# Storing the last pair of token blocks by column halves on three queues, with its last quarter scaled on VectorE

## The chip, the cores and the metric

The kernel runs on one core of a Trainium2 chip. The metric is device time in microseconds (us). It exceeds the span of the profile, which runs from the first to the last instruction, by about 1.7 us. Runs spread over about half a microsecond.

In the traces TensorE is PE and runs the matmuls; VectorE is DVE and ScalarE is ACT, which do the arithmetic on their results; GpSimd is POOL and SyncE is SP. A store is a DMA, a copy to memory. SyncE, ScalarE and GpSimd each start DMAs from a queue of their own. An *issue* is the time for which starting one holds that engine; a store *lands* when its data has arrived; its *flight* here counts from the start of the issue to the landing. "+0.42" is 0.42 us after the end of the last matmul.

## The reference

```python
def _attn_ref(q, k, v, phi):          # batch 8, heads 8, seq 576, head_dim 64, 32 memory slots
    ...                               # softmax of phi makes k_m and v_m; softmax of q k_m^T; times v_m
def _moe_ref(x, w_a, w_b, w_out):     # x: 4608 tokens x 512
    a = x @ w_a
    b = x @ w_b
    return (a * b @ w_out).astype(np.float32)   # 4608 x 512 f32
```

Only the end matters here: the product with `w_out`, its scaling, and the stores of the result.

## The kernel before

Two blocks of 128 tokens are multiplied with `w_out` together, in seven products of half size. They leave four quarters of 128 x 256: left and right columns of block one (`o1`) and of block two (`o2`). `store` sends a block as two halves of 64 rows, each a DMA of its own. For the last pair (`ends`) block two already goes by column halves.

```python
def store(o_sb, cidx, cs=slice(0, d_model), engines=(nc.sync, nc.sync)):
    pair, c = divmod(cidx, NI)
    for z in range(2):
        slot = 2 * c + z
        engines[z].dma_start(out=out_rows[2 * pair + slot // NI, slot % NI, :, cs], in_=o_sb[64 * z:64 * z + 64, cs])
...
        plus(o1[:, NH:], v, u2)                     # quarter 1: block one, right (VectorE)
...
        plus(o2[:, NH:], y, u5)                     # quarter 2: block two, right
        if ends:
            store(o2, cidx + 1, slice(NH, d_model))
...
        plus(o1[:, :NH], x, u1)                     # quarter 3: block one, left
        store(o1, cidx)
...
        nc.scalar.mul(out=o2[:, :NH], in_=y, mul=scale)   # quarter 4: block two, left
        if ends:
            store(o2, cidx + 1, slice(0, NH), (nc.sync, nc.scalar))
```

The softmax here doesn't subtract the row's maximum and nothing guards it: scores larger than these inputs give would overflow.

## Time and profile before

| | before |
|---|---|
| time, median | 247.86 us (247.41 to 247.93) |
| span of the profile | 246.2 us |
| TensorE busy | 95% of the span |
| last matmul ends | 241.4 us |
| last quarter ready | 241.85 us |
| SyncE's last store issued | 243.08 us |

The rows to compare are the last two: a store waits 1.23 us for its turn on a queue while its data lies ready. The prediction shows the lines. The chain of waits on the page does not show this, because it ends at the last compute instruction.

### The profile page before, as it was taken

The numbers are of one execution on the slowest core, as the hardware profiler recorded it, in microseconds if no ns is written. First come the engines' busy times: TensorE is split into PE (matmuls) and PEld (weight loads), VectorE is DVE, ScalarE is ACT, GpSimd is POOL, SyncE is SP. The second block draws the span as 40 slices with busy tenths as digits, with TensorE's granted clock in tenths as the row PEclk, the third lists the DMA queues.
The fourth block names the chain that finished last, engine by engine and source line by source line (L and its number), as shares of the span: only waits on it lengthen the run. The fifth ranks groups of instructions, "written<-read, shape, count | busy, mean of one in ns | idle before, by whom it ended". The sixth has DMA issues, their size and how long they took to land.

```text
span 246.2 us, 7624 instructions
## 1 busy us (share of the span) xinstructions
PE 233.1 (95%) x3016; PEld 165.7 (67%) x3016; DVE 168.6 (68%) x405; ACT 158.6 (64%) x410; POOL 152.8 (62%) x124
## 2 busy tenths in 40 slices
PE   7589999999998999999999999999999999999992
PEld 2334574456665857777787777877787878888881
DVE  3454784468959968876994559865996586756651
ACT  2364772678697489578856768587856867465430
POOL 8734263499799028892899759892849087946000
PEclk9855999999999999999999999999999999999999
DMA  6999999999969804973159832696120303033253
GB/s 202 209 197 207 209 254 206 256 217 284 225 174 209 165 3 105 235 134 88 27 137 216 184 85 44 160 201 160 35 53 3 85 12 77 19 72 75 45 129 95
DMA packets 26035, 33.81 MB, mean 137 GB/s; under 512 B 1936, under 2 KB 20368, under 8 KB 26000
## 3 DMA queue, kind: packets, MB, share of 16 engines
q0 software_dynamic: 19280, 22.71, 50.5%
q1 hardware_dynamic: 6368, 9.97, 16.3%
q10 hardware_dynamic: 352, 0.66, 0.7%
q8 instruction: 23, 0.38, 0.6%
q14 instruction: 12, 0.10, 0.1%
HBM read 42.47 MB, written 9.44 MB: 211 GB/s over the span
## 4 chain that ended last, share of the span: by engine, by line
PE 89%; DVE 3%; DMA 3%; ACT 2%; issue 1%; DVEq 0%
PE pa L584 21%; PE pb L594 19%; PE py L462 16%; PE pv L462 8%; PE pva L337 6%; PE po L389 5%; PE px L462 4%; DMA phi_sb<-in_phi_dram 3%; PE pkv L213 2%; PE pD L314 2%; PE pscore L292 2%; PE pk L256 2%; PE pT L274 1%; PE pT L242 1%; ACT a_sb L587 1%
## 5 line engine op out<-in xcount | busy, mean ns | idle before, releaser
L597 DVE TENSOR_TENSOR ht<-a_sb,pb 128x288 f16<-128x288 f16 x192 | 83.0, 449 | 41.9 <-ACT a_sb L587 28.7
L587 ACT CAST a_sb<-pa 128x288 f16<-128x288 f32 x192 | 75.0, 406 | 31.6 <-PE pa L584 29.3
L584 PE MATMUL pa<-A,vab 128*128 128x288 f16 x384 | 77.4, 291 | 1.6 <-DVE A L325 1.1
L594 PE MATMUL pb<-A,vab 128*128 128x288 f16 x384 | 77.2, 289 | 0.7 <-ACT vab L349 0.5
L444 POOL TENSOR_TENSOR h_sums<-ht 128x768 f16<-128x768 f16 x28 | 45.8, 1639 | 38.8 <-DVE ht L597 37.3
L594 PEld LDWEIGHTS <-vab 128*128 128x128 f16 x384 | 37.5, 99 | 13.4 <-issue 1.7
L584 PEld LDWEIGHTS <-vab 128*128 128x128 f16 x384 | 34.9, 99 | 16.1 <-issue 8.7
L462 PEld LDWEIGHTS <-h_sums 128*128 128x128 f16 x384 | 37.4, 98 | 6.9 <-issue 0.4
L349 ACT CAST vab<-pva 128x512 f16<-128x512 f32 (+1 forms) x52 | 28.0, 559 | 12.0 <-PE pva L337 12.0
L349 DVE CAST vab<-pva 128x512 f16<-128x512 f32 (+1 forms) x52 | 32.6, 643 | 2.9 <-PE pva L337 2.2
L462 PEld LDWEIGHTS <-ht 128*128 128x128 f16 x288 | 28.1, 98 | 5.6 <-issue 0.4
L462 PE MATMUL py<-w_sums,h_sums 128*128 128x256 f16 x192 | 30.3, 272 | 0.0
L444 POOL TENSOR_TENSOR h_sums<-h_sums,ht 128x768 f16<-128x768 f16 x14 | 23.1, 1647 | 1.0
L444 POOL TENSOR_TENSOR h_sums<-ht,h_sums 128x768 f16<-128x768 f16 x14 | 23.0, 1640 | 1.0
L305 ACT ACTIVATE E<-pscore 128x288 f16<-128x288 f32 x32 | 11.4, 417 | 11.3 <-PE pscore L292 11.2
L325 POOL TENSOR_TENSOR A<-E,R 128x576 f16<-128x576 f16 x10 | 12.8, 1275 | 7.1 <-ACT R L323 6.8
L462 PE MATMUL py<-wo_sb,ht 128*128 128x256 f16 x96 | 16.0, 273 | 0.0
L462 PE MATMUL pv<-w_sums,h_sums 128*128 128x256 f16 x96 | 16.0, 272 | 0.0
L469 ACT ACTIVATE u<-py 128x256 f32<-128x256 f32 x32 | 12.4, 387 | 5.2 <-PE py L462 5.0
L462 PE MATMUL py<-w_sums,ht 128*128 128x256 f16 x96 | 15.5, 272 | 0.1
L462 PE MATMUL px<-wo_sb,ht 128*128 128x256 f16 x96 | 15.4, 273 | 0.0
L204 DVE STREAM_TRANSPOSE qT<-q_sb 128x288 f32<-128x288 f32 x32 | 14.3, 462 | 0.6 <-DMA q_sb<-in_q_dram 0.6
(62 smaller groups left out, 262.7 us busy)
## 6 DMA issues: line engine op xcount, KB each, us to landing
out_dram<-o_sb SPq DMA_DIRECT2D x70, 128.0 KB, 2.6
kv_sb<-in_v_dram POOLq DMA_DIRECT2D x7, 576.0 KB, 10.4
phi_sb<-in_phi_dram POOLq DMA_DIRECT2D x7, 576.0 KB, 4.7
kv_sb<-in_k_dram POOLq DMA_DIRECT2D x7, 576.0 KB, 8.2
q_sb<-in_q_dram POOLq DMA_DIRECT2D x6, 576.0 KB, 13.4
wo_sb<-in_moe_w_out_dram POOLq DMA_DIRECT2D x3, 512.0 KB, 16.3
q_sb<-in_q_dram POOLq DMA_DIRECT2D x4, 288.0 KB, 12.6
wa_sb<-in_moe_w_a_dram POOLq DMA_DIRECT2D x2, 512.0 KB, 14.9
```

The source lines that it names most:

```text
L204: nc.vector.transpose(out=t["qT"][:, hp, :].bitcast(F32), in_=qs[b][:, hp, :].bitcast(F32))
L325: engine.tensor_tensor(out=attn[b][:, g, sl], in0=t["E"][:, g, sl], in1=t["R", g][:, sl], op=ALU.mult)
L337: nc.tensor.matmul(t["pva", lo, z][g][0][32 * j:32 * j + 32, 0:hi - lo], t["kvT"][64 * r:64 * r + 64, 4 + g, M * j:M * j + M], w_sbs[z][64 ...
L349: engine_copy(out=vabs[b][z][:, g, lo:hi], in_=pva[:, 0:hi - lo])
L389: nc.tensor.matmul(po, ht[:, i, P * c:P * (c + 1)], wo_sb[:, i, :], start=(i == 0), stop=(i == NFF - 1))
L444: engine.tensor_tensor(out=out, in0=in0, in1=in1, op=op)
L462: nc.tensor.matmul(po, lhs[:, i], rhs[:, i], start=first and i == 0, stop=i == KH - 1, skip_group_check=not first)
L469: nc.scalar.mul(out=x, in_=po, mul=scale)
L584: nc.tensor.matmul(pa, vab[0][:, g, fs], A[:, g, HALF * hf:HALF * (hf + 1)], start=(g == 0), stop=(g == 1))
L587: nc.scalar.copy(out=a_sb, in_=pa)
L594: nc.tensor.matmul(pb, vab[1][:, g, fs], A[:, g, HALF * hf:HALF * (hf + 1)], start=(g == 0), stop=(g == 1))
L597: nc.vector.tensor_tensor(out=ht[:, i, t0:t0 + HALF], in0=a_sbs[hf - hfs[0]], in1=pb, op=ALU.mult)
```

## The change

Its intent is to shorten the tail after the last matmul. Each quarter leaves as soon as it is ready, no queue has a backlog when the last quarter comes, and ScalarE, which now issues stores, doesn't scale the last quarter. This is the whole diff, with unchanged lines left out at `...`.

```diff
         plus(o1[:, NH:], v, u2)
+        if ends:
+            store(o1, cidx, slice(NH, d_model), (nc.gpsimd, nc.gpsimd))
         ...
         plus(o2[:, NH:], y, u5)
         if ends:
-            store(o2, cidx + 1, slice(NH, d_model))
+            store(o2, cidx + 1, slice(NH, d_model), (nc.sync, nc.scalar))
         ...
         plus(o1[:, :NH], x, u1)
-        store(o1, cidx)
+        if ends:
+            store(o1, cidx, slice(0, NH), (nc.sync, nc.scalar))
+        else:
+            store(o1, cidx)
         ...
-        nc.scalar.mul(out=o2[:, :NH], in_=y, mul=scale)
+        if ends:
+            nc.vector.tensor_scalar(out=o2[:, :NH], in0=y, scalar1=scale, scalar2=None, op0=ALU.mult)
+        else:
+            nc.scalar.mul(out=o2[:, :NH], in_=y, mul=scale)
```

## The prediction

> **What bounds the kernel now.** I read the page first, then the timeline of the last ten microseconds, then the DMA issues one at a time, and last the stretches after the final matmul.
>
> The page's share of busy time and its chain say that TensorE sets the pace through the body.
>
> ```profile
> PE 233.1 (95%) x3016; PEld 165.7 (67%) x3016; DVE 168.6 (68%) x405; ACT 158.6 (64%) x410; POOL 152.8 (62%) x124
> ...
> ## 4 chain that ended last, share of the span: by engine, by line
> PE 89%; DVE 3%; DMA 3%; ACT 2%; issue 1%; DVEq 0%
> ```
>
> The change touches neither a matmul nor anything ahead of the last pair of token blocks. I compared the two programs' instruction order engine by engine: TensorE has the same rows in the same order, and the differences on the others are in the last few instructions. So 240 of the 246.2 us should not move. The page's chain also stops too early for this question: it ends at the last compute instruction (ScalarE's L508), and the stores that follow it are not in it. The timeline has them (columns: start us, length us, engine, line, operation, tiles, count; idle time and its releaser in brackets).
>
> ```profile
> 239.51 0.42 DVE L473 SCALAR_TENSOR_TENSOR o_sb<-pv,u 128x256 f32<-128x256 f32 x1 [1.89 <-ACT u L469]
> ...
> 240.14 0.42 DVE L473 SCALAR_TENSOR_TENSOR o_sb<-py,u 128x256 f32<-128x256 f32 x1 [0.20 <-PE py L462]
> 240.62 0.81 PE L462 MATMUL py<-w_sums,ht 128*128 128x256 f16 x6
> 240.79 0.42 DVE L473 SCALAR_TENSOR_TENSOR o_sb<-px,u 128x256 f32<-128x256 f32 x1 [0.23 <-PE px L462]
> 241.47 0.38 ACT L508 ACTIVATE o_sb<-py 128x256 f32<-128x256 f32 x1 [2.23 <-PE py L462]
> 241.88 0.55 ACTq L451 DMA_DIRECT2D out_dram<-o_sb  x1
> ```
>
> The four quarters of the last pair are ready at 239.93, 240.56, 241.21 and 241.85 us. The span is 246.2, so 4.4 us pass after the last quarter is ready. SyncE's issues, read one by one, say what fills them:
>
> ```profile
> 240.59 0.47 SPq L451 DMA_DIRECT2D out_dram<-o_sb  x1
> 241.10 0.60 SPq L451 DMA_DIRECT2D out_dram<-o_sb  x1
> 241.80 0.54 SPq L451 DMA_DIRECT2D out_dram<-o_sb  x1
> 242.38 0.60 SPq L451 DMA_DIRECT2D out_dram<-o_sb  x1
> 243.08 0.54 SPq L451 DMA_DIRECT2D out_dram<-o_sb  x1
> ```
>
> In order these are the two halves of the right quarter of block two, the two full-width halves of block one, and the first half of the left quarter of block two. Each takes 0.58 to 0.70 us of the sequencer with its gap, except the first at 0.51. Block one was ready at 241.21 but is issued at 241.80 and 242.38. The last quarter was ready at 241.85, but its SyncE half is issued at 243.08, 1.23 us late. Only its ScalarE half went out at once (241.88).
>
> The DMA issues in the last 5.7 us give the time from issue to landing, and the waits of SyncE over the same end say that it is these landings that close the program:
>
> ```profile
> out_dram<-o_sb SPq DMA_DIRECT2D x2, 128.0 KB, 2.4
> out_dram<-o_sb SPq DMA_DIRECT2D x3, 64.0 KB, 2.0
> out_dram<-o_sb ACTq DMA_DIRECT2D x1, 64.0 KB, 2.5
> ...
> SPq L710 <- DMA out_dram<-o_sb: 1.1, 3, 0.5
> ```
>
> So the last one lands at 243.08 + 2.0 = 245.1. The other 246.2 - 245.1 = 1.1 us are SyncE stepping through the remaining completion semaphores and the closing barrier. The end is therefore 241.85 (data ready) + 1.23 (queue of SyncE) + 2.0 (flight) + 1.1 (close). The change can only take from the second term and disturb the third.
>
> **What the Trainium skill says.** "DMA: Bandwidth & Descriptors", section "Issuing engines are not separate DMA queues", says that DMAs from all engines share the same 16 DMA engines and that issuing from several saves the sequencer's time alone. That is just the term in question here, and the trace agrees that it is not small at this place: 1.23 us of 4.4. The same page's "Anatomy of one DMA" gives about 2.0 us of fixed cost; the 64 KB stores of the trace show 2.0 us in all, and 2.5 for the one from ScalarE. "VectorE: DVE Perf Modes", section "Why PSUM operands drop a tier", says an fp32 operand from PSUM runs at 1x. The trace agrees: VectorE's 128x512 and 128x256 PSUM casts take 684 and 421 ns, a slope of 263/256 = 1.03 ns per column. "SBUF — State Buffer", section "SBUF: two separate sides", warns that a two-port VectorE operation starves descriptor writing on GpSimd. VectorE's operations at 239.5 to 241.9 have an operand in PSUM, so I expect none; no trace shows it yet.
>
> **The change part by part.**
>
> 1. *Block one, right quarter, to GpSimd.* Ready at 239.93, two issues from 239.96. GpSimd's issues in this trace take about 0.75 us each, so they are done near 241.5. For the load of phi issued at 155.70, the packet records show the first data 1.55 us after the issue's start. So data at about 241.5 and 242.3. For a SyncE store of 64 KB the packets take 0.45 us and the semaphore 0.35 more, so my estimate is a landing by 243.1: not last. GpSimd is otherwise idle there.
>
> 2. *Block two, right quarter, over SyncE and ScalarE.* Both issue at 240.59. SyncE is free at 241.06 in place of 241.70.
>
> 3. *Block one, left quarter, over both.* Ready at 241.21, issued at about 241.24 on both and done at 241.8. The wait of 0.59 us goes, and a full-width 2 x 128 KB becomes 2 x 64 KB here.
>
> 4. *The last quarter scaled on VectorE.* ScalarE took 0.38 us. VectorE should take 0.42: that is what the 128x256 f32 combination and the 128x256 cast from PSUM both take. It costs 0.04 us, and the data is ready at 241.89. What it avoids is ScalarE standing in its own way: its issue of part 3 holds its sequencer until 241.8, and the scaling could not start at 241.47.
>
> 5. *The last two issues.* Both at about 241.92, in place of 243.08 on SyncE. The issue is 1.16 us earlier.
>
> If flight and close stayed at 2.0 and 1.1, the span would fall by 1.16 us. But flight will not be 2.0 for both halves. The bytes are the same 512 KB in less time, and two 64 KB pieces arrive at once: by the packet records one 1 KB packet takes some 0.07 us, so 64 packets on 16 engines are 0.28 us, and two pieces side by side add about 0.2 to the later. And ScalarE's store landed 2.5 us after issue, not 2.0; its first packet came 1.7 us after the issue against SyncE's 1.1. At the start of the kernel the same pair of queues, both issued at 0.81 us, had first packets at 1.93 and 2.72, so ScalarE is again the later by 0.8. With 2.5 for its half the last landing is 241.92 + 2.5 = 244.4 and the gain 245.1 - 244.4 = 0.7 us. I take 0.7 as the middle: 247.86 - 0.7 = 247.1 us after rounding down.
>
> **Rivals.**
>
> *Free queues.* ScalarE's 2.5 was only contention with block one's 2 KB packets: the stretch 243.5 to 244.1 shows the DMA full.
>
> ```profile
> 243.50:244.10 0.60, 0.00 (x0) 0.00 (x0) 0.00 (x0) 0.00 (x0) 0.00 (x0) 1.00 1.05 321
> ```
>
> (The last two columns are the DMA share and GB/s.) Then both halves land about 2.1 us after issue, at 244.0, and the gain is 1.05: 246.8 us. Against it is the kernel's start, where ScalarE was late as well. I give it 3 in 10.
>
> *One descriptor maker for both queues.* If the two queues are served one after the other, each at the 0.55 to 0.65 us that back-to-back issues show, six stores from 240.59 need as long as six on SyncE alone. The last lands near 245, and the gain is 0.2: 247.6 us. For it is the kernel's start, 0.8 us between the two. Against it is the present end, where ScalarE's first packet (243.6) and the next SyncE one (243.8, by the records) are only 0.2 apart. I give it 2 in 10.
>
> *GpSimd as the last to land.* If software descriptors need over 3.5 us, its second half, issued near 240.75, lands at 244.3 or later and the gain shrinks to 0.5 or none. GpSimd's loads land 4.3 us and more after issue, but those are 576 KB each behind others; the first data came at 1.55. I give it 1 in 10.
>
> **Range and chances.** The cases give 246.8, 247.1, 247.6 and near 247.4; the three runs of before spread over 0.52 us. So 246.5 to 247.6. A change of 2% is 5 us. Nothing after the last matmul can give that, since only 4.8 us lie there and over 3 are flight and close. Nothing that is added is longer than 1 us. Within 2%: 0.98.
>
> **What would show it right or wrong.** In the changed profile the tail's matmuls stay where they are. VectorE has a 128x256 operation of 0.42 us starting at the last matmul's end. SyncE has three 64 KB issues, the last starting within 0.1 us of that operation's end, and ScalarE three at the same times. GpSimd has two near 240.0 and 240.7. ScalarE's time to landing stays near 2.5 and SyncE's near 2.0. It is wrong if SyncE's last issue comes later than 0.2 us after the data, if ScalarE lands at 2.0 or above 3.0, if a GpSimd landing is the last wait, or if the span's end moves apart from the last landing.

## The result, and the profile after

The changed kernel took 246.98 us in the median (246.89 to 247.5, four runs), against 247.9 (247.41 to 247.94, four runs) of before. The ratio is 0.9975, with a 95% interval of 0.996 to 0.9989. Ratios are not quite the ratio of the medians or means given beside them. Executions over 1.5% slower than the fastest of the same kernel are left out of the means. In means the gain is 247.79 - 247.09 = 0.70 us.

The timeline of the changed kernel's tail answers to the one in the prediction (start us, length us, then what ran; x2 and x3 are issues merged into one row).

```profile
239.86 1.17 POOL L451 DMA_DIRECT2D out_dram<-o_sb  x2 [14.64 <-DVE o_sb L473]
240.22 2.03 ACTq L451 DMA_DIRECT2D out_dram<-o_sb  x3
240.24 0.81 PE L462 MATMUL py<-w_sums,ht 128*128 128x256 f16 x6
240.42 0.42 DVE L473 SCALAR_TENSOR_TENSOR o_sb<-px,u 128x256 f32<-128x256 f32 x1 [0.23 <-PE px L462]
241.09 0.42 DVE L514 TENSOR_SCALAR o_sb<-py 128x256 f32<-128x256 f32 x1 [0.25 <-PE py L462]
```

GpSimd and ScalarE now carry stores, and the last quarter is a VectorE operation of 0.42 us where ScalarE took 0.38. SyncE's three issues and ScalarE's last, read one at a time:

```profile
240.21 0.47 SPq L451 DMA_DIRECT2D out_dram<-o_sb  x1
240.87 0.47 SPq L451 DMA_DIRECT2D out_dram<-o_sb  x1
241.54 0.47 SPq L451 DMA_DIRECT2D out_dram<-o_sb  x1
...
241.70 0.55 ACTq L451 DMA_DIRECT2D out_dram<-o_sb  x1
```

The last quarter is ready at 241.09 + 0.42 = 241.51. SyncE issues its half 0.03 us later, not 1.23. ScalarE's comes 0.16 after that. The DMA view of the last 6.9 us of the changed kernel (KB each, median us from issue to landing):

```profile
out_dram<-o_sb SPq DMA_DIRECT2D x3, 64.0 KB, 2.2
out_dram<-o_sb ACTq DMA_DIRECT2D x3, 64.0 KB, 2.6
...
out_dram<-o_sb POOLq DMA_DIRECT2D x2, 64.0 KB, 2.2
```

All three medians are above the 2.0 us that SyncE's 64 KB stores took before. The stores now overlap, and part of the gain goes back there.

To compare kernels I count from the end of the last matmul in the trace (241.43 us before, 241.05 after). The landing is the last of the 16 counts of a store's completion semaphore in the trace. The "close" is the time from the last landing to the end of the span.

| us after the last matmul | before | changed | difference |
|---|---|---|---|
| last quarter ready | +0.42 | +0.46 | +0.04 |
| last issue | +1.65 (SyncE) | +0.65 (ScalarE) | -1.00 |
| last landing | +3.65 | +2.88 | -0.77 |
| close | 1.16 | 1.22 | +0.06 |
| end | +4.81 | +4.10 | -0.71 |

The tail gives 0.71 us, which is what the mean times moved. The expectations below say +4.79 and +4.08, because they count from the chain's 241.45 and 241.07, 0.02 us later. The last matmul itself ended 0.38 us earlier in the changed kernel's profile. No part of the change reaches so far back; I come to this with the repeats.

### The profile page after: what moved, and what is told of

Its sections match the earlier page's. It is cut to its first block, busy times and chain, and to the rows that moved or that the text cites. A ratio compares the mean times of both kernels' runs of the same rounds, so it can differ in the third digit from the quotient of the medians.

```text
span 245.2 us, 7629 instructions
## 1 busy us (share of the span) xinstructions
PE 232.1 (95%) x3016; PEld 165.1 (67%) x3016; DVE 168.9 (69%) x406; ACT 158.2 (65%) x409; POOL 154.0 (63%) x126
## 4 chain that ended last, share of the span: by engine, by line
PE 82%; DMA 11%; DVE 3%; issue 1%; ACT 1%; POOL 1%; DVEq 0%; POOLq 0%
PE pa L592 19%; PE pb L602 18%; PE py L462 17%; PE pv L462 8%; DMA wb_sb<-in_moe_w_b_dram 7%; PE pva L337 5%; PE po L389 5%; DMA kv_sb<-in_v_dram 4%; PE px L462 4%; PE pkv L213 2%; PE pD L314 2%; PE pscore L292 1%; PE pT L242 1%; PE pk L256 1%; POOL q_sb L90 1%
```

## The experiments

Twelve experiments ran, nine new kernels and three repeats; every trace passed through the same count from its last matmul. All but e9 gave correct results. Only tails are compared for single runs; where times are given, they are fast runs, but for e1's slow one and e12's single one, whose state is unknown.

### e1: the last quarter back on ScalarE

```diff
-            nc.vector.tensor_scalar(out=o2[:, :NH], in0=y, scalar1=scale, scalar2=None, op0=ALU.mult)
+            nc.scalar.mul(out=o2[:, :NH], in_=y, mul=scale)
```

> The changed kernel with the last quarter scaled on ScalarE again. All times are counted from the end of the last matmul, which in the changed kernel is followed by the data at +0.44, the two last issues at +0.47 (SyncE) and +0.63 (ScalarE), the last landing at +2.87 and the end of the span at +4.08 us. Theory (the issue of block one's last piece, 0.73 us on ScalarE, holds the scaling): scaling starts at about +0.55 in place of +0.02, data at +0.93, both issues near +0.96, last landing +3.2 to +3.4, end +4.4 to +4.6, so 0.3 to 0.5 us longer than the changed kernel and still 0.2 to 0.4 shorter than before (+4.79). Rival (which engine scales makes no odds, 0.38 against 0.42 us): end +4.05.

ScalarE's timeline in e1:

```profile
244.99 1.39 ACTq L451 DMA_DIRECT2D out_dram<-o_sb  x2
246.48 0.38 ACT L514 ACTIVATE o_sb<-py 128x256 f32<-128x256 f32 x1 [2.85 <-PE py L462]
246.89 0.50 ACTq L451 DMA_DIRECT2D out_dram<-o_sb  x1
```

Its two issues hold ScalarE until 246.38. The last matmul ended at 245.82, so the scaling starts at +0.66 (0.11 later than expected) and not at +0.04. The last landing is +3.27 and the end +4.48, or 0.38 us more than the changed kernel. The theory holds for the tail. The profile fell in a slow run (252.04 us). That run's loss lies ahead of the last matmul, and all the tail's issues up to the scaling stand within 0.01 us of the changed kernel's. The three fast runs (246.82 to 247.48, ratio 0.9976) don't resolve 0.4 us.

### e2: only the scaling moved

The kernel before, with this alone:

```diff
-        nc.scalar.mul(out=o2[:, :NH], in_=y, mul=scale)
+        if ends:
+            nc.vector.tensor_scalar(out=o2[:, :NH], in0=y, scalar1=scale, scalar2=None, op0=ALU.mult)
+        else:
+            nc.scalar.mul(out=o2[:, :NH], in_=y, mul=scale)
```

> The kernel before with nothing changed but the last scaling, which goes to VectorE. Theory (SyncE's queue of five issues sets the end): data at +0.44 in place of +0.40, SyncE's last issue still at +1.63, last landing +3.6, end +4.8 us after the last matmul, as before (+4.79). Rival (freeing ScalarE is what shortened the tail): end +4.1 to +4.5.

VectorE and SyncE in e2's timeline:

```profile
241.52 0.42 DVE L509 TENSOR_SCALAR o_sb<-py 128x256 f32<-128x256 f32 x1 [0.25 <-PE py L462]
...
242.43 1.24 SPq L451 DMA_DIRECT2D out_dram<-o_sb  x2
```

The quarter is ready at 241.94. SyncE's last issue starts at 243.12 by the trace, 1.18 us later (1.23 before), and ends at 242.43 + 1.24 = 243.67. The last landing is +3.64 and the end +4.80, as before (+4.81). VectorE brings nothing by itself. It is needed only because ScalarE's queue is used for more stores.

### e3: no GpSimd

The changed kernel, with two queues:

```diff
-            store(o1, cidx, slice(NH, d_model), (nc.gpsimd, nc.gpsimd))
+            store(o1, cidx, slice(NH, d_model), (nc.sync, nc.scalar))
```

> The changed kernel with block one's right quarter on SyncE and ScalarE, so two queues with four issues each. Quarters become ready 0.65 us apart and an issue takes 0.47 to 0.73 us, so by the theory of issue time both queues just keep up: end +4.0 to +4.2 us after the last matmul, the same as the changed kernel (+4.08); GpSimd brings nothing. Rival (two queues of 0.6 to 0.7 us an issue cannot keep up, the third is needed): the backlog grows by 0.05 to 0.1 us an issue, last issues near +0.9, end +4.4 or more. Second rival (the two hardware queues share one maker of descriptors): eight pieces at 0.6 us from -1.5, the last data near +4.4, end +5.5.

The end came at +3.81, earlier than any of the three expected: 0.29 less than the changed kernel. The time is 246.54 us in the median (ratio 0.9944, interval 0.9928 to 0.9961). The DMA view of the end of e3 (SyncE's first store lies ahead of the window):

```profile
out_dram<-o_sb ACTq DMA_DIRECT2D x4, 64.0 KB, 2.1
out_dram<-o_sb SPq DMA_DIRECT2D x3, 64.0 KB, 1.9
```

Set beside the 2.6 and 2.2 of the changed kernel, the flights are shorter by 0.5 and 0.3. The bytes are the same, but block one's right quarter is issued 0.03 us after it is ready, where GpSimd needed 0.29. It has landed by +0.76; GpSimd's pieces landed at +0.81 and +1.89, in the midst of the others. Of the 0.29 us, 0.17 are the earlier last landing (+2.71 against +2.88) and 0.12 a shorter close (1.10 against 1.22), which e7 explains. The two queues keep up, though ScalarE's last issue is at +0.68. Queues that shared one maker of descriptors would have ended at +5.5, so that rival has fallen. The later start and the software queue went together; no run tells how much of the 0.17 us each of them cost.

### e4: column halves on one queue

```diff
-            store(o1, cidx, slice(NH, d_model), (nc.gpsimd, nc.gpsimd))
+            store(o1, cidx, slice(NH, d_model), (nc.sync, nc.sync))
...
-            store(o2, cidx + 1, slice(NH, d_model), (nc.sync, nc.scalar))
+            store(o2, cidx + 1, slice(NH, d_model), (nc.sync, nc.sync))
...
-            store(o1, cidx, slice(0, NH), (nc.sync, nc.scalar))
+            store(o1, cidx, slice(0, NH), (nc.sync, nc.sync))
```

> The changed kernel with all column halves but the very last 64 KB (which stays on ScalarE) on SyncE: seven issues there. Theory (SyncE's issue time is the term): from -1.5 us at about 0.6 us each the seventh starts at about +2.1 to +2.3, lands 2.0 later, end near +5.4 us after the last matmul, 0.6 longer than before (+4.79), so column halves alone make it slower. Rival (smaller pieces and the early start of block one's right quarter are the gain): end +4.1 to +4.6.

SyncE's timeline in e4:

```profile
240.19 4.30 SPq L451 DMA_DIRECT2D out_dram<-o_sb  x7
```

Seven issues fill 4.30 us with gaps of 0.1 us at most, 0.61 each. The seventh starts at +2.30 and lands at +4.28; the end is +5.32, or 0.51 later than before. This shows most directly that issue time is the term: same quarters, same pieces, same VectorE, and the tail goes from +3.81 (e3) to +5.32 by the queue alone.

### e5: GpSimd carries the last piece

On e3:

```diff
-            store(o2, cidx + 1, slice(0, NH), (nc.sync, nc.scalar))
+            store(o2, cidx + 1, slice(0, NH), (nc.gpsimd, nc.scalar))
```

> The kernel without GpSimd's two stores (e3: last landing +2.71, end +3.81 us after the last matmul), but with SyncE's half of the last quarter issued by GpSimd. In the changed kernel GpSimd's closing DRAIN ended 3.4 us after the start of its last issue, though that store had landed 0.87 us before. Theory A (the drain follows GpSimd's last issue by a fixed 3.3 to 3.5 us): issue at +0.49, drain until +3.8 to +4.0, the closing barrier can start only then, end +4.5 to +4.7. Theory B (the drain waits for the landing alone or is only shown long): landing +2.5 to +2.9, end +3.8 to +4.0.

VectorE and GpSimd in e5's timeline:

```profile
241.21 0.42 DVE L514 TENSOR_SCALAR o_sb<-py 128x256 f32<-128x256 f32 x1 [0.25 <-PE py L462]
241.93 0.59 POOL L451 DMA_DIRECT2D out_dram<-o_sb  x1 [16.59 <-DVE o_sb L514]
```

GpSimd starts 0.30 us after the data, where SyncE needs 0.03. Its store lands at +2.86, ScalarE's at +3.03, and the end is +4.48, so the close is 1.44. In the trace's instruction records GpSimd's closing DRAIN lasts until +3.69, and its next instruction, which collects the other engines for the final barrier, follows at once, though SyncE had been done since +3.42. So A's size came out nearly right (an end of +4.5 to +4.7 was expected) and its rule did not. From the start of its last issue the drain took 3.36, 2.93 and 3.10 us (changed kernel, e5, e8), but from its landing 0.87, 0.83 and 0.83. It follows the landing, by some 0.85 us.

### e6: block one at full width

On e3:

```diff
-        if ends:
-            store(o1, cidx, slice(NH, d_model), (nc.sync, nc.scalar))
...
-            store(o1, cidx, slice(0, NH), (nc.sync, nc.scalar))
+            store(o1, cidx, slice(0, d_model), (nc.sync, nc.scalar))
```

> e3 without the column split of block one: its two halves go full width (128 KB each) on SyncE and ScalarE when its left quarter is ready, so each queue has three issues. Theory (only the number of issues on a queue ahead of the last and its start matter, the bytes in flight little): o2's last issues stay at +0.49 and +0.65 to +0.68, the 256 KB have passed by about +2.0, last landing +2.8 to +2.9, and with the close of 1.16 to 1.22 (two completion semaphores fewer in front) end +3.95 to +4.1, within 0.3 of e3 (+3.81). Rival (the early start of the right quarter is what the gain rests on): the last pieces queue behind block one's 2 KB packets as ScalarE's did before, landing +3.1 or later, end +4.3 or more.

The last landing is +3.05 and the end +4.28. The theory, at +3.95 to +4.1, was wrong by 0.2 and the rival, at +4.3 or more, nearly right, though the landing it gave (+3.1) is not reached either. The last issues stand at +0.49 and +0.64 as expected, but the flights are 2.18 and 2.41 in place of 1.93 and 2.04. Bytes in flight count for more than I had thought: the early column half is worth 0.34 us of landing on two queues. The other 0.12 is the close, with two stores fewer ahead of the last (see e7). Without the early half, two queues and VectorE's scaling still give 4.81 - 4.28 = 0.53 us against before.

### e7: two more stores far from the end

On e3:

```diff
+        elif cidx == PAIRED[-4]:
+            store(o1, cidx, slice(0, NH))
+            store(o1, cidx, slice(NH, d_model))
         else:
             store(o1, cidx)
```

> e3 with one block of an earlier pair, stored long before the end, also split by columns, which adds two stores there and moves the last pair's completion semaphores on by two of the eight that are used in turn. In five profiles the close (last landing to end) was 1.22, 1.16, 1.10 and 1.04 us as the last landing came on the second to fifth of the semaphores that SyncE reads one after the other at the end: 0.06 us for each that is still to be read. Theory: the close falls by 0.12 from e3's 1.10 to about 0.98, last landing stays near +2.71, end near +3.69. Rival (the close is a constant and the differences are chance): end +3.8. In the time, 0.1 us is within the spread of runs.

The last landing is +2.72, the close 0.98 and the end +3.70, as the theory has it. At the end SyncE waits for the completion semaphores one after the other in a fixed order, 0.06 us each. What matters is how many still have to be read after the last to arrive. Two stores more, and the last pair falls on later ones. (The trace has the last landings of the five profiles on the third to sixth of the eight; the expectation counts one short.) The time is 246.45 us in the median (ratio 0.9942).

### e8: one store on GpSimd, to free ScalarE

On e3:

```diff
-            store(o2, cidx + 1, slice(NH, d_model), (nc.sync, nc.scalar))
+            store(o2, cidx + 1, slice(NH, d_model), (nc.sync, nc.gpsimd))
```

> e3 with one of ScalarE's stores (second half of block two's right quarter) on GpSimd, so that ScalarE's sequencer is free when the last quarter is ready. Theory (ScalarE's 0.55 to 0.75 us an issue holds its last issue back by 0.2): its last issue moves from +0.68 to +0.49 and its landing from +2.71 to about +2.5 to +2.55, end +3.65 to +3.7, with GpSimd's drain done by about +2.8. Rival (any packets from GpSimd's queue slow ScalarE's, as in the changed kernel where its first store took 2.90 us to land against 2.22 without): last landing +2.8 or later, end +3.9 or more.

ScalarE's last issue did move to +0.49, but took 0.73 us where it took 0.55, and landed at +2.73 against +2.71. The end is +3.87 (ratio 0.9959). The theory failed: an earlier start was used up by a longer issue. Nor is it quite the rival, whose landing was to be +2.8 or later.

### e9: ScalarE's last store alone

On e8:

```diff
-            store(o2, cidx + 1, slice(0, NH), (nc.sync, nc.scalar))
+            nc.scalar.dma_start(out=out_rows[7, 8, :, 0:NH], in_=o2[64:128, 0:NH])
```

> Wrong on purpose: e8 without SyncE's half of the last quarter, so 64 rows of 256 outputs are never written. In e8 ScalarE's half was issued at +0.49 us together with SyncE's, its issue took 0.73 and it landed 2.23 after issue, SyncE's 1.95. Theory (ScalarE's queue is no slower, its half waits for the other 64 KB on the same 16 DMA engines): alone it takes 1.92 to 1.98, landing +2.4 to +2.47. Rival (ScalarE's queue itself is some 0.3 us slower, as the prediction had it with 2.5): it still lands 2.2 after issue, +2.7.

ScalarE's queue in e9:

```profile
241.64 0.72 ACTq L518 DMA_DIRECT2D out_dram<-o_sb  x1
```

It landed 2.17 us after issue, 0.06 less than with SyncE's half beside it. So the shared engines are not the reason and my theory fell. The rival is right in size, but the line shows another cause here than a slow queue: the issue itself takes 0.72. From the issue's end to landing it is 1.45 us. With that count the quiet stores agree: in e3 SyncE's four take 1.45 to 1.46, and ScalarE's last three 1.47 to 1.48. ScalarE's first does not agree: 1.67 in e3, with an issue of 0.55 and only one SyncE store beside it, and 1.64 to 1.66 in e4 to e9 and e11. So 0.2 us of a later ScalarE is left there that its issue does not hold; its cause is open. The issue takes 0.47 to 0.60 on SyncE and 0.50 to 0.75 on ScalarE. What decides between 0.50 and 0.75 stays open. A store beside it does not, since e9's last issue had none.

### e10, e11, e12: repeats, and the best version

> The changed kernel again, unchanged, for the spread of the tail and for a time on the same chip as the next. Last landing within 0.05 of +2.88, end within 0.05 of +4.08 to +4.10 us after the last matmul. Ratio to before 0.997.

> e7 again (no GpSimd in the tail, two more stores early), as the version to keep. End +3.70 us after the last matmul, 0.4 less than the changed kernel; the time 0.3 to 0.5 us below the changed kernel's and 1.0 to 1.4 below before's, ratio to before 0.9945 to 0.996.

> The kernel before again, for the spread of its tail: last landing within 0.05 of +3.65, end within 0.05 of +4.81 us after the last matmul; the last matmul's own end may differ by some tenths, as it did between before and after (241.45 and 241.07), which the theory puts down to the body and not to the change.

| | last landing | end | time, median (range) | ratio to before |
|---|---|---|---|---|
| e12, before | +3.64 | +4.80 | 248.2 (one run) | |
| e10, changed | +2.94 | +4.15 | 246.97 (246.86 to 247.09) | 0.9968 (0.9955 to 0.9981) |
| e11, as e7 | +2.71 | +3.69 | 246.62 (246.38 to 246.97) | 0.9956 (0.9942 to 0.9971) |

The tails repeat, with e10 0.01 us outside what I had allowed. The best version ends its tail 0.46 us before the changed kernel of the same chip; in the mean of five runs each it is 0.30 faster. The ranges of the times overlap, so this rests on the tails. It beats both kernels there, and uses two queues, not three.

The last matmul ended at 241.43 and 241.69 us in the two profiles of before and at 241.05 and 241.00 in those of the changed kernel. In the other kernels outside the slow run it lay between 240.94 and 241.65. These differences come far ahead of the change. At the 401st of 3016 matmuls the traces of before and changed already stand at 38.73 and 38.38 us, and from there to the last matmul every trace takes 202.67 to 202.71 us, but for e12 (202.85) and e1's slow run (206.97). The four traces with all but one store of the tail on SyncE (before, e2, e4, e12) are the latest outside the slow run, which I can't explain; but the mean times moved by 0.70 and, in e10, by 0.79 us (247.77 - 246.98), against 0.71 and 0.65 of the tails. So the times need little or nothing from the body: a tenth of a microsecond or so, which is left open.

## Why the prediction was right

The time and the mechanism were right: 0.7 us forecast, 0.71 in the tail and 0.70 in the means. That they agree to 0.01 is partly luck, since two terms of the sum missed in opposite directions. Point by point:

- *SyncE's queue was the term.* Right. Its wait of 1.23 us became 0.03. e4 brings the wait back, and e2 shows that VectorE alone leaves it in place.
- *VectorE's scaling costs 0.42, and avoids ScalarE standing in its own way.* Right to 0.01 us. e1 shows the second half: undone, it costs 0.38 of the 0.71.
- *Both last issues at the same moment.* Off by 0.16 for ScalarE. Its issue of block one's piece took 0.73 us, not the 0.55 that I read from the only one in the tail of before, and held the next.
- *ScalarE's store lands 2.5 us after issue, because its queue is later.* This step was oversized (2.24, against 2.22 for SyncE's beside it) and right in cause only in part. In before, 2.50 was 0.55 of issue and 1.95 after it. e2 and e4 take the 1.95 apart. Each has a single ScalarE store in its tail, issued at +0.49 in 0.55 us: beside block one's 2 KB packets (e2) it lands 1.92 us after its issue's end, beside 1 KB packets (e4) 1.65. So some 0.3 us was crowding, as the rival "free queues" had it, and 0.2 the later first store on ScalarE (see e9). The last store on ScalarE is the third there in the changed kernel, and in e3, where nothing crowds it, the last lands in 2.04. The two misses together gave 0.65 + 2.24 = 2.89 against 0.47 + 2.5 = 2.97 us after the last matmul, so they nearly cancelled.
- *SyncE's flight of 2.0 will stretch.* Right; it was 2.22. (The prediction's list of signs still has it near 2.0.)
- *The close stays at 1.1.* It was 1.22 against the 1.16 of before in the same count. e7 shows that it depends on which semaphore comes last; the prediction had taken it as fixed.
- *GpSimd is not last to land, so it is harmless.* The first half is right: its second store landed at +1.89. The second is wrong. Its stores started 0.29 us after the data, not 0.03, and flew in among the rest. (There was no sign of VectorE starving GpSimd's descriptor writing: its issues took 0.57 to 0.60 us, less than the 0.75 of its loads, which are larger, and its first packets came 1.17 us after the issue.) ScalarE's half of block two's right quarter took 2.90 us to land, against 2.23 in e3. Without GpSimd the tail is 0.29 shorter, 0.12 of it the close. I did not ask what a transfer that isn't last does to those that are.
- *One maker of descriptors for both queues.* Fell with e3. Its sum was also off: six issues of 0.55 to 0.65 us from 240.59 put the sixth at 243.3 to 243.8 and its landing at 245.3 or later, so no gain and not 0.2. Likewise the rival "GpSimd as the last to land": a landing at 244.3 would still leave a gain of 0.8.

## What to carry to other kernels

When a trace shows data ready and the last stores issued one by one, look to the issue time of that queue: here it set the tail, and a second queue of the same kind took it away. Give the last compute step to an engine that issues nothing. Send early pieces as soon as they are ready, so that they are gone when the last ones fly, and try the last microseconds without GpSimd's queue; here that was worth 0.29 us (e3). A term called fixed, like the close, is worth a look across several traces.

## What the Trainium skill lacked or had wrong

- "DMA: Bandwidth & Descriptors", "Issuing engines are not separate DMA queues", calls the sequencer's time "usually small relative to the DMA itself". For 64 KB stores it was 0.47 to 0.75 us of issue against 1.45 from the issue's end to a quiet landing, and by the queue alone the tail went from +3.81 (e3) to +5.32 (e4).
- The same page's "Latency and other measured facts" has a later first byte on the software path (about 1 us) than on the hardware one (about 0.6 us), and doesn't say from where it counts. From the start of the issue the first packets came after 1.17 us on GpSimd in the changed kernel and 1.12 on SyncE in before, so hardly a difference. GpSimd's drawback was elsewhere: 0.29 to 0.30 us from ready data to its issue, against 0.03.
- No page that I read tells that GpSimd's closing DRAIN ends 0.83 to 0.87 us after its last store has landed, and that the final barrier waits for it (e5: close of 1.44 us).
- No page that I read tells that the completion semaphores are read one by one at a kernel's end in this program, at 0.06 us each, so that the close was 0.98 to 1.22 us by which one arrives last.
